# X loads as single SyncE transfers, four issued at the start, and the gate matrix loaded into its blocks

## The chip, the core and the metric

The kernel runs on one core of a Trainium2 chip. The core has five engines that run their own instruction streams and wait for each other by semaphores: TensorE (PE) for matmuls, VectorE (DVE), ScalarE (ACT), GpSimd (POOL) and SyncE (SP). SP, ACT and POOL can issue DMA transfers; 16 DMA engines of the core carry them out. PE, DVE and the other engines take their instructions in program order, so an instruction that waits holds back all that stand behind it on its engine.

The metric is the device time of one execution in microseconds (us), as a median of several runs. "Granted clock" is the share of full TensorE clock that the chip gave.

## The reference

The input x has 8 sequences of 3584 positions with 192 channels (28672 tokens). A causal convolution with seven taps per head comes first, its taps a softmax of a small weight; then a routed feed-forward network with 8 experts, in which tokens go to experts greedily by their logits, each expert taking exactly 3584:

```python
w = softmax(weight, axis=-1)                       # 8 heads x 7 taps
out = np.einsum('hk,bskhg->bshg', w, x_unf)        # causal: six zeros ahead of each sequence
x = out.reshape(B * S, D)
logits = x @ w_gate                                # 28672 x 8
order = np.argsort(-logits.flatten())
# walk the order: a token takes expert e if it has none yet and e has room
for e in range(E):
    h = np.maximum(x[assigned == e] @ w1[e], 0.0)
    out[assigned == e] = h @ w2[e]
```

## The kernel before

The convolution is done in 16 half batches (`NHB`) of 1792 positions. A half batch's input is the tile X: 118 partitions by 16 windows by 192 channels in float32. Partitions 6 to 117 hold the 112 positions of each window, partitions 0 to 5 the six positions ahead of it (the halo). For each of 8 heads `conv` multiplies X by a banded 118 x 128 matrix `TH`, which `toeplitz` builds from the softmaxed taps on DVE, ACT and POOL at the start; PE writes the product into one of four PSUM banks (`cv`), ACT copies it into the tile `a` (three buffers), and ACT then issues the store of `a` to `attn` in DRAM (L205).

X has four buffers. `load(i)` (L183) fetches half batch i: on POOL a memset of the first window's halo where a sequence begins, on SP the halo (L189 or L192), and then the 112 positions in two halves of eight windows each (L194). Windows 0 to 7 are issued by SP, windows 8 to 15 by ACT (by SP for half batch 0). A load waits until the convolution that read its buffer is done. In the main loop `load(i + 3)` stands ahead of `conv(i)`, so ACT meets the issue of its half ahead of the evictions of half batch i.

The gate: DVE transposes `a` into `aT` (`transp`), PE multiplies it by the gate matrix (`logits`, six steps of four matmuls, two steps at a time under the name `gate`), and ACT copies the result, after a transpose on PE, into `LT` (`logits_t`). The gate matrix lies in GF (shown as c_mu in the profile): 128 partitions by 6 blocks of 32 columns, in which the 32 partitions of quarter pb use columns 8 pb to 8 pb + 7 and the rest is zero. `gate_ops` (L167) loads the matrix four times into `wgr` with one transfer for each quarter, sets GF to zero on POOL, and copies the quarters in with four POOL copies (L173).

The order of work is written out by hand. Inside `conv(i)`, after each head's matmul, `mid(h)` takes one piece from a list: in half batch 2 and later these are, in turn, a quarter of the transposes of half batch i - 1 and two logits steps of half batch i - 2. So the first gate matmuls stand on PE after the second head of half batch 2. On SP the order at the start is: taps, load 0, load 1 (the call inside `toeplitz`, after the exponential, so that ACT's half comes behind it), the four gate transfers, load 2, and from the main loop load 3, load 4 and so on. On POOL the constants of `r.consts()` stand behind the four copies into GF.

From the fourth half batch on, the threshold search and the routing of tokens run on DVE and PE between the convolutions; when lists of tokens exist, POOL gathers rows of `attn` and the feed-forward network begins. It fills the rest of the time, with PE as its main engine.

Of the kernel before, what the change touches and what calls it, by code (L numbers as in the profile page):

```python
# [6 lines left out]
F32 = mybir.dt.float32  # L7
# [8 lines left out]
NE, D, NTOK, F, CAP = 8, 192, 28672, 1024, 3584  # L16
W, HW_, NHB = 112, 16, 16
# [97 lines left out]
def build(ctx, tc, nc, x, weight, wg, attn, LT, wk):  # L115

    k = K()
    k.nc = nc
    k.tc = tc
    V, A, PE, P = nc.vector, nc.scalar, nc.tensor, nc.gpsimd  # L120
    cst = ctx.enter_context(tc.tile_pool(name="cst", bufs=1, side="right"))


    wb = cst.tile([128, 8, 7], F32, name="wb")
    nc.sync.dma_start(wb, bass.AP(tensor=weight.tensor, offset=weight.offset, ap=[[0, 128], [7, 8], [1, 7]]))
    pmi = cst.tile([128, 128], I32, name="pmi")
    P.iota(pmi, pattern=[[-1, 128]], base=0, channel_multiplier=1)
    D0 = cst.tile([128, 128], BF, name="D0")
    V.tensor_copy(D0, pmi)
    TH = cst.tile([128, 8, 128], F32, name="TH")  # L130
    P.memset(TH[:, :, W:128], 0.0)
    MK = cst.tile([128, 7, W], BF, name="MK")
    for j in range(7):
        V.tensor_scalar(MK[:, j], D0[:, 0:W], float(j), None, op0=OP.is_equal)
    wm = cst.tile([128, 8], F32, name="wm")

    def toeplitz():
        V.tensor_reduce(wm, wb, axis=AX.X, op=OP.max)
        V.tensor_tensor(wb, wb, wm[:, :, None].to_broadcast([128, 8, 7]), op=OP.subtract)
        A.activation(wb, wb, AF.Exp)  # L140
        load(1)
        V.tensor_reduce(wm, wb, axis=AX.X, op=OP.add)
        V.tensor_scalar(wm, wm, 1e-9, None, op0=OP.add)
        V.reciprocal(wm, wm)
        V.tensor_tensor(wb, wb, wm[:, :, None].to_broadcast([128, 8, 7]), op=OP.mult)

        tk = cst.tile([128, 2, W], F32, name="tk")
        for h in (1, 5):
            A.activation(TH[:, h, 0:W], MK[:, 0], AF.Copy, scale=wb[:, h, 0:1])
            for j in range(1, 7):  # L150
                A.activation(tk[:, j % 2], MK[:, j], AF.Copy, scale=wb[:, h, j:j + 1])
                P.tensor_tensor(TH[:, h, 0:W], TH[:, h, 0:W], tk[:, j % 2], op=OP.add)
        for hs in ((0, 2), (3, 4), (6, 7)):
            for j in range(7):
                for h in hs:
                    t = TH[:, h, 0:W]
                    if j == 0:
                        V.tensor_scalar(t, MK[:, 0], wb[:, h, 0:1], None, op0=OP.mult)
                    else:
                        V.scalar_tensor_tensor(t, MK[:, j], wb[:, h, j:j + 1], t, op0=OP.mult, op1=OP.add)  # L160


    wgr = cst.tile([128, 6, 8], F32, name="wgr")
    GF = wk.tile([128, 6, 32], F32, name="c_mu")
    pm = wk.tile([128, 1], F32, name="pm")

    def gate_ops():  # L167
        for pb in range(4):
            nc.sync.dma_start(wgr[32 * pb:32 * pb + 32], wg.rearrange("(c f) e -> f c e", f=32))
        P.memset(GF, 0.0)  # L170
        for pb in range(4):
            q = slice(32 * pb, 32 * pb + 32)
            P.tensor_copy(GF[q, :, 8 * pb:8 * pb + 8], wgr[q])  # L173

        pi = cst.tile([128, 1], I32, name="pi")
        P.iota(pi, pattern=[[0, 1]], base=0, channel_multiplier=1)
        V.tensor_scalar(pi, pi, 24, None, op0=OP.bitwise_and)
        V.tensor_scalar(pm, pi, 24.0, -1.0, op0=OP.is_equal, op1=OP.mult)


    X, AT, AA = {}, {}, {}

    def load(i):  # L183
        t = X[i] = k.xp[i % 4].tile([118, 16, D], F32, name="X")
        b, hf = divmod(i, 2)
        o = x.offset + (b * 3584 + hf * 1792) * D
        if hf == 0:
            P.memset(t[0:6, 0], 0.0)
            nc.sync.dma_start(t[0:6, 1:16], bass.AP(tensor=x.tensor, offset=o + (W - 6) * D,  # L189
                                                    ap=[[D, 6], [W * D, 15], [1, D]]))  # L190
        else:
            nc.sync.dma_start(t[0:6], bass.AP(tensor=x.tensor, offset=o - 6 * D, ap=[[D, 6], [W * D, 16], [1, D]]))  # L192
        for eng, w in ((nc.sync, 0), (A if i else nc.sync, 8)):
            eng.dma_start(t[6:118, w:w + 8], bass.AP(tensor=x.tensor, offset=o + w * W * D, ap=[[D, W], [W * D, 8], [1, D]]))  # L194

    def conv(i, mid):
        t = X.pop(i)
        a = AA[i] = k.ap[i % 3].tile([128, 16, D], F32, name="a")
        o = a.rearrange("p w (h c) -> p h w c", c=24)
        for h in range(8):  # L200
            ps = k.cps.tile([128, 512], F32, name="cv")
            PE.matmul(ps[:, 0:384], TH[0:118, h], t[:, :, h * 24:(h + 1) * 24], start=True, stop=True)
            mid(h)
            A.activation(o[:, h], ps[:, 0:384].rearrange("p (w c) -> p w c", c=24), AF.Copy)
        A.dma_start(attn[i * 1792:(i + 1) * 1792].rearrange("(g p b) d -> p g (b d)", g=4, b=4),  # L205
                    a[0:W].rearrange("p (g b) d -> p g (b d)", b=4))

    def transp(i, u):

        if u == 0:  # L210
            AT[i] = [k.hp[i % 2].tile([128, 16, 6, 32], F32, name="aT")]
        V.transpose(AT[i][0][:, 4 * u:4 * u + 4].rearrange("p w c t -> p (w c t)"),
                    AA[i][:, 4 * u:4 * u + 4].rearrange("p w d -> p (w d)"))
        if u == 3:
            AA.pop(i)

    def logits(i, u):

        if u == 0:
            AT[i].append(k.bank("pl"))  # L220
        pl = AT[i][-1]
        for c in range(4):
            w = slice(4 * c, 4 * c + 4)
            PE.matmul(pl[32 * c:32 * c + 32, 0:128], GF[:, u], AT[i][0][:, w, u], start=(u == 0), stop=(u == 5))
        if u == 5:
            L = AT[i] = k.lrow()
            l, m = (t.rearrange("p (w t) -> p w t", t=32) for t in (L, pl[:, 0:128]))
            A.activation(l[:, :, 0:16], m[:, :, 0:16], AF.Copy)
            A.activation(l[:, :, 16:32], m[:, :, 16:32], AF.Identity, bias=pm)

    def logits_t(i):
        L = AT.pop(i)
        pt = k.bank("pt")
        PE.transpose(pt[:, 0:128], L, k.ident)
        v = pt[:, 0:128].rearrange("p (b q e) -> p e b q", q=4, e=8)
        o = LT[:, :, 16 * i:16 * i + 16].rearrange("p e (b q) -> p e b q", q=4)
        A.activation(o, v, AF.Copy)

    k.load, k.conv, k.transp, k.logits, k.logits_t = load, conv, transp, logits, logits_t
    k.toeplitz, k.gate_ops = toeplitz, gate_ops  # L240
    return k

# [1241 lines left out]
def moe_kernel(ctx, tc, x, weight, wg, w1, w2, out):  # L1484
    nc = Pace(tc.nc)
    V, P = nc.vector, nc.gpsimd
# [4 lines left out]
    with ExitStack() as cw:  # L1491
# [71 lines left out]
        ff.xg = pool(cw, "fg", 2)  # L1563
        ff.xs = pool(cw, "fx", 2)
        k = build(cs, tc, nc, x, weight, wg, attn, LT, wk)
        k.ident = r.ident
        lp = pool(cs, "lp", 2, **right)
# [41 lines left out]
                for _ in range(2):  # L1609
                    todo.pop(0)()  # L1610

        k.load(0)
        k.toeplitz()
        k.gate_ops()
        k.load(2)
        r.consts()
        for i in range(NHB):
            if i + 3 < NHB:
                k.load(i + 3)
            if i == 4:  # L1620
                r.consts_late()
            if i == 13:
                cx[0].close()
                for _ in range(4):
                    ff.wload()
                ff.wpool(cw, 0, **late)

            def mid(h):

                if i and h == 0:  # L1630
                    if i >= LAG:
                        left.append(partial(gates, i - 2))
                    for u in range(4):
                        left.append(partial(k.transp, i - 1, u))
                        if 1 < i and (u == 3 or i < LAG):
                            left.append(partial(gate, i - 2, u) if u < 3 else partial(end, i - 2))
                for _ in range(2 if got else 1):
                    if left and (i < LAG or got):
                        left.pop(0)()
                if i >= 14 and h % 2:  # L1640
                    ff.wsplit(-1, P)
                hook(8 * i + h)

            k.conv(i, mid)
# [88 lines left out]
```

## Time and profile before

| What | Value |
|---|---|
| Time, median of 3 runs | 1236.66 us (1236.03 to 1237.11) |
| Profiled execution | 1234.62 us |
| Its span, first to last instruction | 1232.9 us |
| Mean granted clock | 0.998 |
| DMA traffic | 182.03 MB, mean 148 GB/s |

The profile is of one execution. Its page gives each engine's busy time and share of the span; "PEld" is PE's weight load, which overlaps PE. The strip of 40 slices gives busy shares in tenths. A row of the timeline reads: start, duration, engine, line, operation, out <- in, shape, how many were merged into the row, and in brackets how long the engine sat idle before it and what ended that wait. SPq and ACTq are the queues from which SP and ACT issue transfers; the duration of such a row is that of the issue, not of the transfer. Many lines are recorded as L56, a helper through which DVE, ACT and PE are called, so instructions are told apart by their tiles.

### The profile page before, as it was taken

How to read it: one execution, taken by the hardware profiler on the slowest of the kernel's cores; microseconds unless marked ns; L12 is line 12 of the kernel's file. 1: busy time of each engine (PE TensorE's matmuls, PEld its weight loads, DVE VectorE, ACT ScalarE, POOL GpSimd, SP SyncE). 2: the span in 40 equal slices, each digit the busy share in tenths (PEclk: the TensorE clock that was granted, in tenths of full speed). 3: DMA queues.
4: the chain of work that ended last, by engine and by line, in shares of the span. 5: the costliest groups of instructions: out<-in, count | busy, mean ns of one | idle time of the engine just before them, and what ended most of it. 6: DMA issues, size and time to landing. Idle time of an engine off the chain costs nothing.

```text
span 1232.9 us, 21779 instructions
## 1 busy us (share of the span) xinstructions
PE 1201.0 (97%) x7694; PEld 1034.1 (84%) x7694; DVE 983.1 (80%) x2117; ACT 565.6 (46%) x1252; POOL 540.3 (44%) x528
## 2 busy tenths in 40 slices
PE   4999999999999999999999999999999999999997
PEld 2445678899989988889888889999999999999997
DVE  7398789898998988899979866777777777777762
ACT  4454565556445455454554443333433343334332
POOL 3000344444546555545455435444444544543422
PEclk9999999999999999999999999999999999999999
DMA  9999674659427474655343432114323232423100
GB/s 239 347 344 326 230 223 123 176 158 312 153 59 220 133 246 129 219 159 190 88 132 114 116 106 74 49 40 152 108 91 105 97 107 89 159 72 120 49 24 28
DMA packets 129221, 182.03 MB, mean 148 GB/s; under 512 B 21632, under 2 KB 91728, under 8 KB 127440
## 3 DMA queue, kind: packets, MB, share of 16 engines
q1 hardware_dynamic: 86496, 104.15, 27.3%
q0 software_dynamic: 21504, 44.07, 12.0%
q10 hardware_dynamic: 21104, 32.34, 7.8%
q8 instruction: 62, 1.02, 0.4%
q14 instruction: 55, 0.45, 0.1%
HBM read 102.38 MB, written 78.12 MB: 146 GB/s over the span
## 4 chain that ended last, share of the span: by engine, by line
PE 91%; DVE 4%; DMA 2%; ACT 1%; issue 1%; POOL 0%; SPq 0%; ACTq 0%; POOLq 0%; DVEq 0%
PE ph L56 42%; PE y L56 41%; PE cv L56 3%; PE bg L56 3%; DMA X<-in_x_dram 1%; DVE aT L56 1%; PE pl L56 1%; DMA wgr<-in_moe_w_gate_dram 1%; DVE X L56 1%; PE px L56 0%; ACT a L56 0%; ACT X L56 0%; POOL c_mu L173 0%; SPq L194 0%; DVE hl L56 0%
## 5 line engine op out<-in xcount | busy, mean ns | idle before, releaser
L56 PE MATMUL y<-w,hh 128*128 128x384 f32 x1792 | 535.8, 355 | 0.0
L56 ACT ACTIVATE hh<-ph 128x512 fp32r<-128x512 f32 x448 | 268.0, 598 | 470.8 <-PE ph L56 467.9
L56 PE MATMUL y<-w,hl 128*128 128x192 f32 x1792 | 449.0, 251 | 0.0
L56 DVE SCALAR_TENSOR_TENSOR hl<-ph,hh 128x512 fp32r<-128x512 f32 x448 | 307.9, 687 | 133.3 <-ACT hh L56 127.4
L56 PE MATMUL ph<-xa,w 128*128 128x512 f32 x1344 | 395.0, 402 | 0.0
L56 PEld LDWEIGHTS y<-w,hl 128*128 128x128 f32 x1792 | 340.9, 190 | 16.3
L56 PEld LDWEIGHTS y<-w,hh 128*128 128x128 f32 x1792 | 336.3, 188 | 19.8 <-issue 1.7
L1367 POOL DMA_INDIRECT out_dram<-yo,ia x128 | 145.4, 1136 | 211.5 <-DVE yo L56 180.6
L56 PEld LDWEIGHTS ph<-xa,w 128*128 128x128 f32 x1344 | 218.4, 189 | 20.3 <-issue 1.2
L1367 POOL DMA_INDIRECT out_dram<-yo,ib x96 | 96.0, 1000 | 220.0 <-DVE yo L56 212.6
L56 PE MATMUL ph<-xd,w 128*128 128x512 f32 x448 | 177.7, 397 | 1.2 <-DVE xd L56 1.2
L56 PE MATMUL ph<-xd,dl 128*128 128x512 f32 x448 | 174.2, 389 | 0.3 <-DVE dl L56 0.3
L56 DVE STREAM_TRANSPOSE xs<-xg 32x128 f32<-32x128 f32 (+2 forms) x408 | 164.8, 404 | 6.6
L1292 POOL DMA_INDIRECT xg<-attn,ja x128 | 140.6, 1098 | 46.2 <-issue 40.7
L56 ACT ACTIVATE yt<-y 128x192 f32<-128x192 f32 x224 | 73.2, 327 | 94.3 <-PE y L56 91.7
L56 PE MATMUL cv<-X,TH 118*128 118x384 f32 x256 | 99.5, 517 | 17.3 <-DVE TH L56 12.7
L1292 POOL DMA_INDIRECT xg<-attn,jb x96 | 103.5, 1078 | 29.3 <-issue 29.0
L56 DVE TENSOR_TENSOR yo<-y,yt 128x192 f32<-128x192 f32 x224 | 79.3, 354 | 42.8 <-ACT yt L56 40.2
L56 PEld LDWEIGHTS ph<-xd,w 128*128 128x128 f32 x448 | 84.0, 188 | 21.5 <-DVE xd L56 1.7
L56 PEld LDWEIGHTS ph<-xd,dl 128*128 128x128 f32 x448 | 84.2, 188 | 19.9 <-issue 0.5
L56 PEld LDWEIGHTS cv<-X,TH 118*128 118x128 f32 x256 | 45.1, 195 | 47.7 <-issue 12.5
L56 ACT ACTIVATE a<-cv 128x384 f32<-128x384 f32 x128 | 59.2, 493 | 47.4 <-PE cv L56 23.0
(238 smaller groups left out, 918.0 us busy)
## 6 DMA issues: line engine op xcount, KB each, us to landing
attn<-a ACTq DMA_DIRECT2D x16, 1344.0 KB, 10.2
X<-in_x_dram SPq DMA_DIRECT2D x17, 672.0 KB, 14.3
raw<-in_moe_w_dram SPq DMA_DIRECT2D x56, 192.0 KB, 4.0
X<-in_x_dram ACTq DMA_DIRECT2D x15, 672.0 KB, 10.5
kw<-w SPq DMA_DIRECT2D x36, 256.0 KB, 4.3
kv<-w SPq DMA_DIRECT2D x24, 384.0 KB, 5.7
scr<-xs SPq DMA_DIRECT2D x96, 96.0 KB, 2.6
w<-kw SPq DMA_DIRECT2D x6, 1536.0 KB, 7.2
```

The lines of the kernel that those rows point to most:

```text
L56: return f(*a, **k)
L1292: self.nc.gpsimd.indirect_dma_start(out=t[:, b], out_offset=None, in_=self.attn[0:rows], in_offset=bass.IndirectOffsetOnAxis(ap=idx[b], ax ...
L1367: st = self.nc.gpsimd.indirect_dma_start(out=self.out, out_offset=bass.IndirectOffsetOnAxis(ap=idx, axis=0), in_=o, in_offset=None, bounds ...
```

## The change

Three things change. A half batch's 112 positions are one transfer of 16 windows, issued by SP, in place of two of eight; ACT issues no load of X any more. Loads 0 to 3 are issued one behind the other before `toeplitz`; in the loop, load 4 comes first, at i = 1. The gate matrix is transferred straight into GF's four blocks, behind the memset of GF; the tile `wgr` and the POOL copies are gone. The four transfers have the same sizes as before and stand on SP behind the four loads.

```diff
@@ toeplitz
         A.activation(wb, wb, AF.Exp)
-        load(1)
         V.tensor_reduce(wm, wb, axis=AX.X, op=OP.add)
@@ gate_ops
-    wgr = cst.tile([128, 6, 8], F32, name="wgr")
     GF = wk.tile([128, 6, 32], F32, name="c_mu")
     pm = wk.tile([128, 1], F32, name="pm")
 
     def gate_ops():
-        for pb in range(4):
-            nc.sync.dma_start(wgr[32 * pb:32 * pb + 32], wg.rearrange("(c f) e -> f c e", f=32))
         P.memset(GF, 0.0)
         for pb in range(4):
-            q = slice(32 * pb, 32 * pb + 32)
-            P.tensor_copy(GF[q, :, 8 * pb:8 * pb + 8], wgr[q])
+            nc.sync.dma_start(GF[32 * pb:32 * pb + 32, :, 8 * pb:8 * pb + 8],
+                              wg.rearrange("(c f) e -> f c e", f=32))
@@ load
-        for eng, w in ((nc.sync, 0), (A if i else nc.sync, 8)):
-            eng.dma_start(t[6:118, w:w + 8], bass.AP(tensor=x.tensor, offset=o + w * W * D, ap=[[D, W], [W * D, 8], [1, D]]))
+        nc.sync.dma_start(t[6:118], bass.AP(tensor=x.tensor, offset=o, ap=[[D, W], [W * D, 16], [1, D]]))
@@ moe_kernel
-        k.load(0)
+        for i in range(4):
+            k.load(i)
         k.toeplitz()
         k.gate_ops()
-        k.load(2)
         r.consts()
         for i in range(NHB):
-            if i + 3 < NHB:
+            if 0 < i and i + 3 < NHB:
                 k.load(i + 3)
```

## The prediction

> **What bounds the kernel now.** I read the page first, then busy time by stage, then the first 60 us row by row.
>
> ```profile
> span 1232.9 us, 21779 instructions
> PE 1201.0 (97%) x7694; PEld 1034.1 (84%) x7694; DVE 983.1 (80%) x2117; ACT 565.6 (46%) x1252; POOL 540.3 (44%) x528
> DMA  9999674659427474655343432114323232423100
> ```
>
> PE works 97% of the span, in program order. A shift of its early work that is not swallowed by a later wait therefore reaches the end at its full size. The change touches the loads of X and the gate matrix only, and these belong to the first stage, where the DMA engines are busy in nine tenths and more. The table by stage says where PE has time to lose there:
>
> ```profile
> 10.00:20.00 10.00, 7.28 (x16) 3.67 (x17) 8.97 (x32) 4.92 (x12) 4.79 (x12) 1.00 1.13 238
> 20.00:30.00 10.00, 7.30 (x22) 3.78 (x20) 7.77 (x15) 4.38 (x10) 2.78 (x17) 0.95 1.09 290
> 30.00:40.00 10.00, 10.00 (x84) 5.28 (x84) 1.98 (x3) 4.00 (x11) 1.78 (x3) 0.88 1.07 359
> 40.00:50.00 10.00, 8.12 (x68) 4.25 (x67) 4.40 (x7) 3.98 (x11) 0.00 (x0) 1.00 1.06 339
> 50.00:60.00 10.00, 10.00 (x87) 5.03 (x85) 5.41 (x7) 6.24 (x16) 0.25 (x1) 1.00 1.05 344
> ```
>
> The columns are the stretch, its length, busy us of PE, PEld, DVE, ACT and POOL, the granted clock, the DMA share and GB/s. PE is short in 10 to 30 and in 40 to 50; in 20 to 40 the clock is granted at 0.95 and 0.88, which is 0.5 + 1.2 = 1.7 us of full clock missing. The PE timeline, then the merged one, name the waits:
>
> ```profile
> 11.51 6.15 PE L56 MATMUL cv<-X,TH 118*128 118x384 f32 x12 [11.51 <-DVE TH L56]
> 18.87 6.69 PE L56 MATMUL cv<-X,TH 118*128 118x384 f32 x20 [1.21 <-DVE TH L56]
> 28.26 2.21 PE L56 MATMUL cv<-X,TH 118*128 118x384 f32 x4 [2.70 <-DMA X<-in_x_dram]
> ```
>
> ```profile
> 30.40 1.08 PE L56 MATMUL pl<-aT,c_mu 128*32 128x128 f32 x16
> ...
> 33.33 2.04 ACT L56 ACTIVATE a<-cv 128x384 f32<-128x384 f32 x5 [7.24 <-DMA attn<-a]
> ...
> 42.93 2.02 ACT L56 ACTIVATE a<-cv 128x384 f32<-128x384 f32 x5 [4.57 <-DMA X<-in_x_dram]
> ...
> 43.47 1.56 PE L56 MATMUL cv<-X,TH 118*128 118x384 f32 x4 [1.88 <-ACT a L56]
> ...
> 48.42 0.65 PE L56 MATMUL pl<-aT,c_mu 128*32 128x128 f32 x16
> ```
>
> Half batches 0 and 1 wait for TH alone and end at 18.87 + 6.69 = 25.56. Half batch 2 then waits 2.70 us for X. At 28.4 ACT stands still until 33.33, and again before 42.93: the next thing in its order is the issue of the other half of an X load, and that waits for an earlier transfer. The second of these stops PE by 1.88 us. One ACT copy into LT closes each half batch of logits, so these rows are the milestones:
>
> ```profile
> 37.70 0.28 ACT L56 ACTIVATE LT<-pt 128x128 f32<-128x128 f32 x1 [0.27 <-PE pt L56]
> 47.24 0.28 ACT L56 ACTIVATE LT<-pt 128x128 f32<-128x128 f32 x1 [0.26 <-PE pt L56]
> 54.83 0.28 ACT L56 ACTIVATE LT<-pt 128x128 f32<-128x128 f32 x1 [0.27 <-PE pt L56]
> 62.41 0.28 ACT L56 ACTIVATE LT<-pt 128x128 f32<-128x128 f32 x1 [0.27 <-PE pt L56]
> ```
>
> An undisturbed half batch takes 54.83 - 47.24 = 7.59 us, and 7.58 again; the one that ends at 47.24 took 9.54. In an undisturbed one it is 54.83 - 48.42 = 6.41 us from the first gate matmul (pl) to the copy. From 47.24 on I take the rest of the kernel as a fixed train.
>
> **Removed and moved, part by part.**
>
> ```profile
> 5.14 6.02 SPq L169 DMA_DIRECT2D wgr<-in_moe_w_gate_dram  x4
> ...
> 12.76 0.26 POOL L170 MEMSET c_mu<- 128x192 f32 x1
> ...
> 16.60 0.27 SPq L189 DMA_DIRECT2D X<-in_x_dram  x1
> ...
> 17.18 0.31 SPq L194 DMA_DIRECT2D X<-in_x_dram  x1
> 17.54 0.46 SPq L192 DMA_DIRECT2D X<-in_x_dram  x1
> 17.57 2.30 POOL L173 COPY c_mu<-wgr 32x48 f32<-32x48 f32 x4 [4.56 <-DMA wgr<-in_moe_w_gate_dram]
> ...
> 18.04 0.57 SPq L194 DMA_DIRECT2D X<-in_x_dram  x1
> ...
> 20.48 3.87 SPq L189 DMA_DIRECT2D X<-in_x_dram  x1
> ...
> 20.96 0.32 ACTq L205 DMA_DIRECT2D attn<-a  x1
> ```
>
> Loads 2 and 3 on SP now stand behind four gate transfers and a wait until 16.60; with the change all four loads are issued first. Load 2 then moves ahead of load 3 and of the gate matrix. Its SP half lands at 28.26 today, when PE takes it. How early can it be?
>
> ```profile
> DMA packets 8198, 5.51 MB, mean 213 GB/s; under 512 B 1105, under 2 KB 8197, under 8 KB 8197
> ...
> X<-in_x_dram SPq DMA_DIRECT2D x3, 67.5 KB
> ```
>
> ```profile
> DMA packets 728, 0.55 MB, mean 238 GB/s; under 512 B 15, under 2 KB 728, under 8 KB 728
> ```
>
> ```profile
> DMA packets 1211, 1.91 MB, mean 375 GB/s; under 512 B 28, under 2 KB 775, under 8 KB 1211
> ...
> q1 hardware_dynamic: 571, 0.43, 29.4%
> ```
>
> These are answers on the DMA queues for 0 to 25.9 us, for 16.5 to 18.8 and for 25.9 to 31 (q1 is SP's). A load is two halves of 672 KB and a halo of 67.5 or 72 KB, 1.45 MB; four are 5.79 MB. At 238 GB/s and a start near 2.6 us, three loads (4.34 MB) need 18.2 us: load 2 is there by 21 to 24 us, before PE ends half batch 1 at 25.56. **The wait of 2.70 us goes.** The two stops of ACT go as well, since no X transfer is left in its order. Alone, this would put the two half batches up to the second LT copy at 25.56 + 1.5 (two heads) + 6.41 + 7.59 = 41.1 instead of 47.24, **6.2 us earlier**.
>
> **What is late next: the gate matrix.** Its four transfers stood ahead of loads 2 and 3 and landed at 17.5, 13 us before their first use at 30.40. Now they stand behind all four loads on SP's queue. The first logits come after two heads of half batch 2, at 25.56 + 1.5 = 27.05, and PE takes everything in order: until GF is there it stands. So the time t at which GF lands decides. From below: in 0 to 25.9 us the kernel moved 5.51 of the 5.79 MB, and the store of half batch 0 (1344 KB, issued 20.96) not yet. The remaining 0.28 MB then ran beside that store at 0.43 MB in 5.1 us, 84 GB/s, so some 3 us more: 29, and with the landing 30. Without any store in front it would be 28. From the landings:
>
> ```profile
> DMA to landing us min/median/max: 11.9/11.9/11.9
> ```
>
> ```profile
> 24.40 18.04 DMA X<-in_x_dram
> ```
>
> The first row is that store alone: 20.96 + 11.9 = 32.9. The second, of the chain of waits, is the next SP load behind load 3, which lands at 42.4. Load 2's half landed at 28.2, so load 3's lies between 28 and 42; the middle is 35. I take **t = 33.5**, next to the store's 32.9, and keep 28 and 37 as ends.
>
> The Trainium skill, "DMA: Bandwidth & Descriptors", section "Why a DMA increments its semaphore by 16 and not by 1", speaks against the change here. By it a transfer from SP runs on as many engines, up to 16, as divide its slowest dimension: 16 for 112 or 32 partitions, 6 for a halo's 6 rows. Six engines would then hold the halo packets of four loads in addition, and a piece of GF behind them. Its estimate here, with rows of 768 bytes and 52 ns each (16 engines at 238 GB/s): 62 rows or 3 us later on those six; by it t is 31 without a store in front and 34 with one. No view here shows single engines, so t stays as chosen.
>
> With a PE wait from 27.05 to 33.5 the clock falls too. Nearest row: after the idle 2.70 us 1.7 us of full clock were missing. I take 1.7; it may be 0 if GF comes early. The same skill, "TensorE: Matmul & The Clock Gate", section "Part 1: The HAM clock gate (the "warmup" mystery)", has half rate after an idle window of about 3.4 us, and 3.4 us of half rate are those 1.7; the trace agrees.
>
> **The sum.** Second LT copy: 33.5 + 6.41 + 7.59 + 1.7 = 49.2 against 47.24, **+2.0 us**.
>
> ```profile
> 96.84 1.89 ACTq L194 DMA_DIRECT2D X<-in_x_dram  x1
> ```
>
> ```profile
> 6.45 5.46 DVE L56 SCALAR_TENSOR_TENSOR TH<-MK,wb,TH 128x112 f32<-128x112 bf16 x12
> ...
> 15.95 3.03 DVE L56 SCALAR_TENSOR_TENSOR TH<-MK,wb,TH 128x112 f32<-128x112 bf16 x12
> ```
>
> Later ACT loses such issues too (1.89 us at 96.84, ahead of an eviction). PE has four banks in hand, so most is hidden; I count -0.5, between 0 and -1.9. The four POOL copies (2.30 us and a wait of 4.56) go, and POOL's constants move from 20 us to 13. There they run beside TH: DVE's TH step took 455 ns (5.46 / 12) beside POOL's additions and 253 without. One to two us of POOL work can cost TH 0 to 1 us, hidden while PE waits for GF; if GF is early it counts. ACT's store of half batch 1 may have to wait for an earlier transfer until about t; its evictions then start near t, when PE has used two of four banks, so nothing is added. Loads 4 on, issued as buffers come free, have about 9 us in hand (load 4's half lands at 42.4 and half batch 4 starts at 47).
>
> In total +1.5 us: 1234.6 becomes 1236.1 for the profiled execution, which lies 2.0 below the median of 1236.66; on the median **1238.2**. In short the change is t - 32.0 us.
>
> **Rivals.**
> 1. *GF lands early* (t below 29.5): the loads run without the store in front, as 5.51 MB by 25.9 us would let them. Against: the store is issued at 20.96, before load 3 ends. At t = 28.5 the clock loss is about 0 and the result is 28.5 + 14.0 - 47.24 - 0.5 = -5.2, 1231.5; at 29.5 it is -2.5, 1234.2. Chance 0.19.
> 2. *GF lands later than the store* (t above 34.5): load 3's tail and GF get turns only beside stores, at 84 GB/s; for it speaks the load that took 18.04 us. At t = 36.5 it is +4.5, 1241.2; it decides from 34.5 on. Slower. Chance 0.26.
> 3. *The change doesn't reorder*: SP is held by earlier transfers (5.14 + 6.02, then until 16.60), so loads 2 and 3 start no earlier and GF lands last all the same; it ends like 2, near 1241, and is in its chance.
>
> My forecast (t 29.5 to 34.5, 1234.2 to 1239.1) has 0.55. A measurement of this kernel can tell about 0.2%, 2.5 us, from no change. The range 1232.3 to 1241.0 leaves out 0.1 on either side, by t from 28.7 to 36.3. Faster 0.19, same 0.55, slower 0.26.
>
> **What would show it.** Half batch 2's first matmuls near 25.6 without a wait for X; a PE wait ended by GF's transfer at the first pl near 33.5, with half clock after it; no ACT wait behind an X issue; the second LT copy near 49.2. Wrong if pl follows at 27 (then the copy is near 41 to 43), if X is still waited for at 28, or if a later stage takes back what the LT copies show.

## The result: 0.96% slower, and the profile after

The changed kernel takes **1248.85 us** (median of 5 runs, 1246.97 to 1249.32) beside 1236.39 us for the kernel before on the same chip (5 runs, 1235.63 to 1237.11). The ratio on record is 1.0096, with a 95% interval of 1.0084 to 1.0107 (dividing the two medians gives 1.0101, inside it). I had forecast 1238.2 us with a range to 1241.0, so the change is slower by more than the whole range allowed. "Before" and "after" are the two kernels below; GF is the gate matrix in its blocks, shown as c_mu.

The page of after says where the traffic went. Its rows: the span, and the DMA queues with packets (rows of a transfer), MB and share of 16 engines' time:

```profile
span 1245.2 us, 21734 instructions
...
q1 hardware_dynamic: 99920, 114.47, 31.4%
...
q10 hardware_dynamic: 7424, 22.02, 4.6%
```

The span is 12.3 us longer than before's 1232.9. SP's queue (q1) carries 114.47 MB; the 22.02 MB on ACT's queue (q10) are the 16 stores of `attn` alone (16 times 1344 KB). Next the timeline of PE in the first 45 us, then that of SP and ACT:

```profile
19.12 8.27 PE L56 MATMUL cv<-X,TH 118*128 118x384 f32 x24 [0.42 <-DVE TH L56]
39.88 1.08 PE L56 MATMUL pl<-aT,c_mu 128*32 128x128 f32 x16 [12.49 <-DMA c_mu<-in_moe_w_gate_dram]
```

```profile
19.14 13.96 SPq L168 DMA_DIRECT2D c_mu<-in_moe_w_gate_dram  x4
...
21.20 0.35 ACTq L200 DMA_DIRECT2D attn<-a  x1
...
26.36 0.31 ACTq L200 DMA_DIRECT2D attn<-a  x1
```

The first row runs through half batch 1 into the first two heads of half batch 2 without a stop: the wait of 2.70 us for X is gone. Then PE stands 12.49 us, until GF lands at 39.88. Both stores (at 21.20 and 26.36) were issued without a stop, 0.35 and 0.31 us each, in front of the last gate pieces, and the issue of the four gate transfers itself took 13.96 us. The table by stage shows the price of the idle time in the clock (columns as above):

```profile
30.00:40.00 10.00, 0.12 (x4) 0.15 (x8) 0.00 (x0) 0.00 (x0) 0.00 (x0) 0.55 1.02 314
40.00:50.00 10.00, 10.00 (x77) 5.15 (x80) 1.19 (x2) 3.80 (x10) 1.59 (x3) 0.77 1.02 193
```

From 40 to 50 the clock is 0.77, so 2.3 us of full clock are missing there. The milestones are the second and the eleventh LT copy and the first matmul of the experts (ph), from the timelines of ACT and PE. First after:

```profile
56.09 0.28 ACT L56 ACTIVATE LT<-pt 128x128 f32<-128x128 f32 x1 [0.27 <-PE pt L56]
...
134.63 0.28 ACT L56 ACTIVATE LT<-pt 128x128 f32<-128x128 f32 x1 [0.27 <-PE pt L56]
...
167.78 0.94 PE L56 MATMUL ph<-xa,w 128*128 128x512 f32 x3
```

and before, whose second copy is at 47.24:

```profile
126.12 0.28 ACT L56 ACTIVATE LT<-pt 128x128 f32<-128x128 f32 x1 [0.26 <-PE pt L56]
...
155.62 0.94 PE L56 MATMUL ph<-xa,w 128*128 128x512 f32 x3
```

The second copy is 56.09 - 47.24 = **8.85 us** later, the eleventh 8.51, ph 12.16, the span 12.3. So two losses make the result: 8.85 us at GF, and 12.16 - 8.51 = **3.65 us** between the eleventh copy and the experts. The chain of work that ended last names the second (first two rows, after), and the timeline of PE shows it as a wait (third row):

```profile
133.29 14.98 DMA raw<-in_moe_w_dram
...
157.41 8.32 DMA xg<-attn,ja
```

```profile
165.78 0.51 PE L56 MATMUL bg<-ident,xg 128*128 128x128 f32 x2 [3.50 <-DMA xg<-attn,ja]
```

These are the experts' weights (raw) and the first gather of tokens (xg), behind the weights' preparation on POOL. SP issues the first raw transfer at 133.29; before it did at 116.00:

```profile
116.00 1.10 SPq L1219 DMA_DIRECT2D raw<-in_moe_w_dram  x1
```

### The profile page after: what moved, and what is told of

Same layout as the page of the kernel before. It is cut to its first block, busy times and chain, and to the rows that moved or that the text cites. A ratio compares the mean times of both kernels' runs of the same rounds, so it can differ in the third digit from the quotient of the medians.

```text
span 1245.2 us, 21734 instructions
## 1 busy us (share of the span) xinstructions
PE 1202.3 (97%) x7694; PEld 1034.5 (83%) x7694; DVE 981.3 (79%) x2117; ACT 566.5 (45%) x1252; POOL 537.8 (43%) x524
## 3 DMA queue, kind: packets, MB, share of 16 engines
q1 hardware_dynamic: 99920, 114.47, 31.4%
q10 hardware_dynamic: 7424, 22.02, 4.6%
## 4 chain that ended last, share of the span: by engine, by line
PE 89%; DVE 5%; DMA 4%; issue 1%; ACT 1%; POOL 0%; SPq 0%; POOLq 0%; ACTq 0%; DVEq 0%
PE ph L56 42%; PE y L56 40%; PE cv L56 3%; PE bg L56 3%; DMA raw<-in_moe_w_dram 1%; DVE aT L56 1%; DVE X L56 1%; DVE TH L56 1%; PE pl L56 1%; DMA attn<-a 1%; DMA xg<-attn,ja 1%; DMA c_mu<-in_moe_w_gate_dram 1%; PE px L56 0%; DMA wb<-in_weight_dram 0%; SPq L189 0%
```

## The experiments

The edits are against the kernel named in each. All ratios are to before, run in the same group on the same chip; in the groups of e5 to e8 and of e17, e18 before itself took 1245 to 1247 us, so times aren't compared between groups, ratios are.

### GF early: e1, e2, e3

e1 takes GF's lateness away: the memset of GF and the four transfers stand behind load 0.

```diff
         for i in range(4):
             k.load(i)
+            if i == 0:
+                k.gate_load()      # memset of GF, four gate transfers
         k.toeplitz()
-        k.gate_ops()               # with the gate transfers
+        k.gate_ops()               # without them
```

> The changed kernel with the four gate transfers (and the memset of GF) moved from behind load 3 to behind load 0. Theory: the late gate matrix cost 8.8 us (second LT copy at 56.09 in place of 47.24), and a second loss of about 3.6 us comes later, where the expert weights arrive late behind SP's loads. Then the first gate matmul follows at about 27.4 with no wait, the second LT copy stands near 41.5, and the time is 1236.4 - 5.7 + 3.6 = about 1234. Rival: the loads themselves are too slow on one queue, PE then waits for load 3 or 4 where it waited for GF, the second LT copy stays above 50 and the time above 1243.

Measured: 1245.05 us, ratio 1.0073 (1.0055 to 1.0091). GF was no longer waited for, yet the second LT copy came at 49.90. In place of GF it is load 3, for half batch 3, that PE waits for (timeline of PE, e1):

```profile
39.28 2.90 PE L56 MATMUL cv<-X,TH 118*128 118x384 f32 x4 [4.93 <-DMA X<-in_x_dram]
```

GF's place in the queue therefore explains only a part. Whatever holds back GF holds back the loads as well.

e2 keeps the change, but loads 4 on go back to two halves, on SP and ACT:

```diff
+        if i < 4:
             nc.sync.dma_start(t[6:118], ...)          # 16 windows
+            return
+        for eng, w in ((nc.sync, 0), (A, 8)):
+            eng.dma_start(t[6:118, w:w + 8], ...)     # 8 windows
```

> The changed kernel, but from load 4 on a half batch comes again as two halves, the second issued by ACT; loads 0 to 3 stay single transfers on SP. Theory: the later loss of 3.6 us comes from SP's queue, which carries all loads and holds the expert weights back (their first issue at 133.3 in place of 116.0); with half the load on ACT the first weight issue is within 10 us behind that of before, the wait of 3.5 us for xg goes, and the time is 1248.9 - 3.6 = about 1245; the wait of 12.5 us for GF stays. Rival: the weights are late only because the whole first stage is late; then the time stays at 1249.

1247.5 us, 1.0099 (1.0081 to 1.0117). The first raw issue moves from 133.29 to 126.54 (timeline of SP, e2):

```profile
126.54 1.33 SPq L1218 DMA_DIRECT2D raw<-in_moe_w_dram  x1
```

The wait for xg is gone, and from the eleventh copy to ph it is 166.16 - 136.66 = 29.50 us, exactly before's 155.62 - 126.12. So the later 3.65 us come from loading X over the one queue. The ratio gains nothing: in the profiles ph is 1.62 us earlier than after's (166.16 against 167.78), as GF came even later (first pl at 41.36 instead of 39.88), and that much the ratios don't tell apart.

e3 has both edits.

> Both edits at once: gate transfers behind load 0, and halves on SP and ACT from load 4 on. Theory: both losses go and the start is 5.7 us earlier than before: 1236.4 - 5.7 = about 1231, below both kernels; ACT's waits ahead of its half loads may return and cost up to 2 us. Rival, one of the losses has another cause: 1234 or more.

1241.69 us, 1.0048 (1.0031 to 1.0064): the wait for GF and the later loss are gone (29.47 us from the eleventh copy to ph), but X of half batch 3 is still 3.61 us late at 38.34, and ACT's stops are back.

### One part at a time: e4 to e8

e4 is before with the single transfer alone, on SP.

```diff
-        for eng, w in ((nc.sync, 0), (A if i else nc.sync, 8)):
-            eng.dma_start(t[6:118, w:w + 8], ...)
+        nc.sync.dma_start(t[6:118], ...)
```

> The kernel before, with one part of the change alone: a half batch's 112 positions are one transfer on SP, in the order of before, gate copies as before. Theory: the queue on SP makes the expert weights late by several us (+3.6) and ACT's two stops go (-1.9): about 1238. Also load 2 stands behind the gate transfers on SP, so half batch 2 waits for X until 28 or later. Rival: which queue carries the second half makes no difference to the weights; then about 1235.

1243.15 us, 1.0056 (1.0039 to 1.0073). More than half of the loss is in this part alone. Timeline of PE, then the answers on the DMA queues for 30 to 34 us and for 44 to 49 us:

```profile
38.17 2.90 PE L56 MATMUL cv<-X,TH 118*128 118x384 f32 x4 [4.61 <-DMA X<-in_x_dram]
```

```profile
q10 hardware_dynamic: 483, 1.43, 88.8%
q1 hardware_dynamic: 250, 0.19, 14.0%
```

```profile
DMA packets 1360, 1.03 MB, mean 206 GB/s; under 512 B 19, under 2 KB 1360, under 8 KB 1360
```

While a store is under way, the loads get 0.19 MB in 4 us, 47 GB/s. When it has passed, the loads run alone, at 206 GB/s. The total swings between some 400 and 206.

e5 is the change with halves everywhere; e6 is before with the gate straight into GF; e7 is e4 with the transfer split in two again, both on SP; e8 has whole transfers, even half batches on SP, odd ones on ACT.

```diff
# e6, in before's place
+        P.memset(GF, 0.0)
         for pb in range(4):
-            nc.sync.dma_start(wgr[32 * pb:32 * pb + 32], ...)
+            nc.sync.dma_start(GF[32 * pb:32 * pb + 32, :, 8 * pb:8 * pb + 8], ...)
-        P.memset(GF, 0.0)          # and the four POOL copies
# e7
+        for w in (0, 8):
+            nc.sync.dma_start(t[6:118, w:w + 8], ...)
# e8
+        (A if i % 2 else nc.sync).dma_start(t[6:118], ...)
```

> The changed kernel with every half batch as two halves again, the second on ACT (on SP for half batch 0): the four early loads and the direct gate transfer stay. Theory of the order: the gate transfers stand last behind four loads and a store, whatever the size of the loads; then the first gate matmul stays near 36 to 39, the second LT copy near 53 to 56, and the time at 1243 to 1246. Rival, the single transfers make the loads slow: the gate matrix lands by 33, the second LT copy near 48, about 1237.

> The kernel before with the direct gate transfer alone: the four transfers go into GF's blocks in the place of the old ones, behind the memset of GF at 13. Theory: the matrix is in place by about 20, its first use is at 30.4, and SP waits until 16.6 anyway: 1236.5, within 1 us. Rival: the later issue on SP pushes loads 2 and 3 back by 3 us or more, half batch 2 starts at 30 or later, 1238 to 1240.

> The kernel before, with both halves of eight windows issued by SP, one behind the other. It tells apart why the single transfer alone came to 1243.2. Theory of the queue: one queue carries all loads, its issues are held until earlier loads are in, and less is in flight: the time is again about 1243, with waits for X at half batch 3 and later. Rival, the size: a transfer of 16 windows is slow in itself; then halves on SP give about 1236.

> The kernel before, with one transfer of 16 windows for a half batch, issued by SP for even and by ACT for odd half batches. Theory of the queue: two queues share the load again, so the waits for X go and the time is 1235 to 1238. Rival, the size: about 1243 again.

| Kernel | Time, us | Ratio | 95% interval |
|---|---|---|---|
| e5 | 1254.98 | 1.0076 | 1.0056 to 1.0096 |
| e6 | 1247.95 | 1.0019 | 1.0008 to 1.0030 |
| e7 | 1253.11 | 1.0057 | 1.0040 to 1.0074 |
| e8 | 1247.58 | 1.0019 | 1.0007 to 1.0031 |

e7 equals e4: two small transfers on SP cost what one large one does. e8 has the large transfers and gives two thirds of the loss back. So it isn't the size of the transfer but **which queue** the loads stand in. e5 never waits for GF, but PE begins only at 21.78 instead of 11.51. ACT's halves of three more loads stand beside load 0: from 2 to 10 us SP's queue, with load 0 in it, moved 417 rows and ACT's 1514. That PE waits for load 0 is argued from this, as the trace names DVE; so e5 doesn't separate the theories. In e6 SP can issue the gate only after POOL's memset (at 12.72 instead of 5.14), and load 2 behind it comes late (SP's half is issued at 18.19 instead of 17.18):

```profile
30.16 2.90 PE L56 MATMUL cv<-X,TH 118*128 118x384 f32 x4 [4.11 <-DMA X<-in_x_dram]
```

### What stands in front of GF: e9, e10, e12

e9 is the change with the stores of half batches 0 and 1 issued behind half batch 2; e10 is the change without the halo transfers of loads 1 to 3, so that part of the convolution at the borders of windows is left out; e12 is before with the gate straight into GF, the memset early and load 2 ahead of the gate.

```diff
# e9: conv
-        A.dma_start(attn[i * 1792:(i + 1) * 1792]..., a[0:W]...)
+        ST.append((i, a))
+        while ST and i > 1:
+            j, s = ST.pop(0)
+            A.dma_start(attn[j * 1792:(j + 1) * 1792]..., s[0:W]...)
# e10: load, and P.memset(X[i][0:6], 0.0) for i in 1 to 3 behind gate_ops
+        if 0 < i < 4:
+            pass
-        if hf == 0:
+        elif hf == 0:
# e12
         load(1)
+        load(2)
...
         k.gate_ops()
-        k.load(2)
```

> The changed kernel with the stores of half batches 0 and 1 issued only behind half batch 2, so that no store is in front of the gate transfers. Looked at: the start of the first gate matmul, 39.9 in the changed kernel. Theory: two stores of 1344 KB, each some 3.5 us of all DMA engines, were served ahead of load 3's tail and of the gate matrix, where I had counted one; without them it starts at 32 to 34. Rival: four loads on one queue take that long by themselves; then 37 or later. The total is no aim here, since half batch 3 then waits for the late stores.

> The changed kernel without the halo transfers of loads 1 to 3, whose six partitions are set to zero on POOL instead; this leaves out part of the computation at the borders of windows of those half batches. Looked at: the first gate matmul. If the halos' rows lie on a few of the 16 DMA engines, and these finish last, 47 rows of about 52 ns go from the slowest ones and it starts 2.5 us or more earlier, at 37 or below. If the halos are spread evenly (216 of 5655 KB), it moves by less than 1 us.

> A version that is meant to beat both: the kernel before with halves on both queues, the gate matrix straight into GF (memset of GF first of all), and only load 2 moved ahead of the gate transfers, its second half issued by ACT behind that of load 1. Theory: half batch 2 starts at 25.6 without a wait for X, the gate matrix is there by 25, ACT's stops remain, the second LT copy is 2 to 4 us earlier than before: ratio 0.997 to 0.9985. Rival: load 3 is later for it, half batch 3 waits, and the ratio is 1.000 or more.

In e9 the gate comes 39.88 - 34.22 = 5.7 us earlier (timeline of PE). The second row is e9's strip of busy DMA engines in tenths, 40 slices of 20 to 30 us:

```profile
34.22 1.08 PE L56 MATMUL pl<-aT,c_mu 128*32 128x128 f32 x16 [6.50 <-DMA c_mu<-in_moe_w_gate_dram]
```

```profile
DMA  9999999999999999999999999999999999864543
```

The two stores thus cost GF 5.7 us. And even with no store at all in flight, the engines are busy for only three to five tenths from 29 to 30 us. That the end of the loads and the gate hang on a few engines would fit this; no view shows single engines. In total e9 gains nothing (1248.92 us, a single run), as the held stores come all at once and ACT waits for them later.

e10 has no wait for GF at all. Answers on the DMA queues for 2 to 20 us, of after and of e10:

```profile
DMA packets 5166, 3.86 MB, mean 214 GB/s; under 512 B 172, under 2 KB 5166, under 8 KB 5166
```

```profile
DMA packets 5794, 4.34 MB, mean 241 GB/s; under 512 B 176, under 2 KB 5794, under 8 KB 5794
```

and for 30 to 40 us of after, 20 to 30 us of e10:

```profile
DMA packets 3005, 3.14 MB, mean 314 GB/s; under 512 B 850, under 2 KB 2370, under 8 KB 3005
...
q10 hardware_dynamic: 667, 1.95, 48.2%
```

```profile
DMA packets 3397, 2.99 MB, mean 299 GB/s; under 512 B 869, under 2 KB 2953, under 8 KB 3396
```

The gate matrix is the only large group of pieces below 512 bytes in these stretches (4 times 32 x 6 pieces of 32 bytes, 768 in all; a few others are always there), so the count of those packets shows when it moved: in e10 before 30 us, in after nearly all behind 30, together with 1.95 MB of stores. Without the halos the loads ran at 241 GB/s instead of 214 and at 20 us only some 1.2 of their 5.6 MB were left, against 1.9 of 5.8 in after; these and the gate were through before 30 us, ahead of the second store. With the halos the loads were not through when the two stores came, and the gate's pieces moved beside and behind the stores. The gain is far more than the expected 2.5 us. But e10 is no clean test of the halos: its memsets hold POOL for 8.12 us, PE waits 3.44 us for TH, and the stores are issued at 23.05 and 29.90 instead of 21.20 and 26.36. How much of it is due to the halos, and how much to the later stores, is open. e10's time is 1241.29 us (a single run); from the eleventh copy to ph it is 161.93 - 129.34 = 32.6 us, so the later loss remains.

e12 takes 1242.66 us, 1.0046 (1.0031 to 1.0060): with load 2 ahead of the gate PE waits for ACT's evictions instead, 4.92 us at 27.86. ACT stands 6.42 us until 27.32: ahead of those evictions it has the store of half batch 0 to issue, at 23.56, and its half of load 4, at 26.95, which by the chain of waits was held by its half of load 3 (issued at 11.58).

### Rows of the stores: e11, e13 to e16

A store row has 3072 bytes (four windows of a position), a load row 768 bytes. e11 is e4 with stores in rows of 768 bytes. It leaves the index of the gather as it was, so that the experts get other tokens' rows.

```diff
-        A.dma_start(attn[i * 1792:(i + 1) * 1792].rearrange("(g p b) d -> p g (b d)", g=4, b=4),
-                    a[0:W].rearrange("p (g b) d -> p g (b d)", b=4))
+        A.dma_start(attn[i * 1792:(i + 1) * 1792].rearrange("(w p) d -> p w d", w=16), a[0:W])
```

> The kernel with single transfers on SP alone (1.0056 of the time before), with stores whose rows in DRAM are 768 bytes in place of 3072; the rows of attn then stand in another order, so that the gathers fetch other positions. Theory: stores take turns with loads row by row, a store row is four load rows, so a store passes quickly and the loads then run alone, at 215 to 250 GB/s, where mixed with stores the total is 340 to 375; with equal rows they mix longer and the waits for X shrink: ratio 1.000 to 1.003. Rival: one queue of loads is slow whatever stands beside it: 1.005 or more.

1232.33 us, 0.9955 (0.9939 to 0.9972): faster than before, where e4 was 0.56% slower. From e13 on the index for the gather goes with the order (the token's own number, which takes two short DVE instructions fewer a list, not three as the expectation says):

```diff
-        V.scalar_tensor_tensor(y, i, -127.0 / 4, x, op0=OP.mult, op1=OP.add)
...
-        V.scalar_tensor_tensor(y, gi, 28.0, y, op0=OP.mult, op1=OP.add)
...
-        V.scalar_tensor_tensor(y, i, 4.0, y, op0=OP.mult, op1=OP.add)
+        V.scalar_tensor_tensor(y, i, -80.0, x, op0=OP.mult, op1=OP.add)
...
-            V.tensor_scalar(row, y, 4.0, None, op0=OP.mult)
+            V.tensor_scalar(row, y, 0.0, None, op0=OP.max)
```

e13 is before, e14 after, e15 e4 and e16 e3, each with these small rows.

> Before, with attn kept in the order of the tokens: a half batch's store has 1792 rows of 768 bytes in place of 448 of 3072, and the index for the gather is the token's own (three short DVE instructions fewer in each list). Theory R (row by row turns): before's loads ride half on SP's and half on ACT's queue, where the stores stand in order with them, and its traffic from 30 to 120 us already ran at 340 GB/s; so little is to be had: ratio 0.996 to 1.000, 30 to 120 us at 335 to 350 GB/s, the wait of 2.70 us for X at half batch 2 gone or changed by up to 2 us. Theory Q (the one queue): before has no such queue and the rows do nothing: 0.999 to 1.001. A price of small rows (1792 descriptors of 768 bytes for a store): slower, 1.001 to 1.006, and the store's landing some us later.

> The whole change with the same small store rows and matching indices. Theory R: the two stores no longer go ahead of the four loads and the gate transfers whole, so GF lands a few us earlier (first pl without a wait or with under 8 us, where it was 13.40 to 14.66), traffic from 30 to 120 us back from 303 to 330 GB/s or more, LT copy 10 to first ph back from 35.3 to 31.7 us; ratio 0.996 to 1.003. Theory Q: first pl at 39 to 40 and the later 3.65 us stay: 1.008 to 1.010.

> e11 again (before with the single transfer on SP, small store rows), now with indices to match, so that the expert stage gathers the rows that the reference asks for. Theory R: as e11, ratio 0.994 to 0.998, 30 to 120 us at about 341 GB/s, second LT copy at about 45. If e11's gain came from its other gathers in the expert stage: 1.002 to 1.006, as e4, with the stage before 140 us as in e11.

> The change with the gate transfers behind load 0, loads 4 on as halves on SP and ACT (as e3, 1.0048) and the small store rows with matching indices. Theory R: its X wait at half batch 3 (3.61 us) and ACT's stops shrink, ratio 0.994 to 1.000. Theory Q: as e3, 1.003 to 1.006.

| Kernel | Loads | Large rows | Small rows, ratio (interval) |
|---|---|---|---|
| before, e13 | halves on SP and ACT | 1 | 1.0144 (1.0126 to 1.0162) |
| after, e14 | whole on SP, four first | 1.0096 | 1.0037 (1.0023 to 1.0051) |
| e4, e15 | whole on SP | 1.0056 | **0.9938** (0.9925 to 0.9952) |
| e3, e16 | halves from load 4 on | 1.0048 | 1.0176 (1.0154 to 1.0198) |

Where the loads stand on SP alone, small rows win 0.6 to 1.2%. Where half of them stand on ACT's queue with the stores, small rows lose 1.3 to 1.4%. Answers on the DMA queues of e15 for 30 to 34 us, the stretch shown for e4 above:

```profile
DMA packets 1923, 1.48 MB, mean 369 GB/s; under 512 B 20, under 2 KB 1922, under 8 KB 1922
...
q1 hardware_dynamic: 961, 0.73, 53.9%
q10 hardware_dynamic: 961, 0.73, 53.8%
```

961 rows of loads and 961 rows of the store in the same 4 us: here the queues take turns **row for row**. Not in every stretch: from 28 to 30 us it was 275 rows of loads to 700 of the store, and in e4's stretch above 250 to 483. What sets the turns there is open; from 30 to 120 us e15 has 20974 rows of loads to 19880. With equal rows the loads get half here, 0.73 MB in 4 us or 183 GB/s, and the engines are hardly ever left with loads alone: the two queues together still move 347 GB/s over 30 to 120 us. A load row takes an engine 0.539 * 16 * 4 us / 961 = 36 ns here; in e4's stretch of loads alone it was 62 ns (1.054 * 16 * 5 us / 1360, its q1 had 105.4%). A half batch's load and store (2.75 MB without the halo) thus need 7.5 us at 369 GB/s, just the 7.59 us that PE takes for one. In e4 they need 1.38 MB at 358 GB/s for the store (1.43 MB in 4 us) and, after the 0.18 MB that pass beside it, 1.2 MB at 206: by this estimate 9.7 us. That is more than PE's pace, and the loads fall behind until PE's own half batches grow to some 10 us.

e14 shows which loss goes: GF is still waited for, 12.16 us until 39.81, but from the eleventh copy to ph it is 163.00 - 133.89 = 29.11 us again. In e15 it is 28.89 us, so the other index is worth at most 0.6 us there; its second copy is at 40.79, 6.45 us ahead of before's (timeline of ACT, e15):

```profile
40.79 0.28 ACT L56 ACTIVATE LT<-pt 128x128 f32<-128x128 f32 x1 [0.27 <-PE pt L56]
```

The Trainium skill, "DMA: Bandwidth & Descriptors", section "Queues, rings and completion order", says that each engine goes round the queues for which it has work, a packet of several descriptors at a time; the equal counts of 30 to 34 us agree, the 275 to 700 of 28 to 30 us don't show it. The same page of the Trainium skill, "Issuing engines are not separate DMA queues", says that issuing from several engines saves only issue time; here e7 and e8, with 1.0057 and 1.0019, differ by more than that, and the measurement decides.

e13 answers the other half. Timeline of ACT, and the list of PE's waits in the first 180 us:

```profile
21.29 5.82 ACTq L194 DMA_DIRECT2D X<-in_x_dram  x1
27.16 1.64 ACT L56 ACTIVATE a<-cv 128x384 f32<-128x384 f32 x4 [6.58 <-DMA X<-in_x_dram]
```

```profile
PE cv L56 <- ACT a L56: 18.9, 8, 5.1
```

ACT's issue of its half of a load takes 5.82 us right behind the store of half batch 0. The same row of before:

```profile
21.40 0.43 ACTq L194 DMA_DIRECT2D X<-in_x_dram  x1
```

That is 0.43 us. The store's 1792 rows in place of 448 stand ahead of it in ACT's own queue. ACT's evictions wait meanwhile, and PE for them, 18.9 us in eight waits. That the queue has no room left for so many rows is argued from this, not shown.

### What is left of the change: e17, e18

e17 is e1 with small rows; e18 is e15 with e6's gate.

> The change with the gate transfers behind load 0 (as e1) and the small store rows with matching indices (as e14). If GF's place and the rows of the stores are the whole loss: no wait for GF, LT copy 10 to first ph 29 us, ratio 0.992 to 0.998, as e15. If the order of the four loads, begun ahead of all, costs something of its own (load 3 lands late, X waits as the 4.93 us in e1): second LT copy at 47 or later, ratio 0.999 to 1.004.

> e15 (single transfers on SP, small store rows, before's order) with the gate transfers straight into GF behind its memset, in before's place. If the direct transfers do harm by themselves (e6: +0.19%, half batch 2 waits 4.11 us for X as the memset holds SP back): 0.995 to 0.998. If small store rows cover it: 0.993 to 0.995.

e17: 1240.28 us beside 1246.64, 0.9953 (0.9938 to 0.9967). e18: 1239.38 us, 0.9947 (0.9934 to 0.9960). In e17 half batch 2 waits 3.27 us for X, and the second copy is at 45.56. Timeline of PE and of ACT, e17:

```profile
28.51 1.53 PE L56 MATMUL cv<-X,TH 118*128 118x384 f32 x4 [3.27 <-DMA X<-in_x_dram]
```

```profile
45.56 0.28 ACT L56 ACTIVATE LT<-pt 128x128 f32<-128x128 f32 x1 [0.27 <-PE pt L56]
```

All of the change's edits are in e17, with the gate's transfers moved and the stores in other rows, and it is 0.47% faster than before. So with GF's place and the rows of the stores altered, nothing of the loss is left. (From the eleventh copy to ph e17 and e18 have 32.4 us instead of 29.5, but so do e6 and e8, with 33.0, on runs where before was slower too; there is no profile of before from those, so the reason is open.) The order of the four loads, and the gate without its POOL copies, show no gain of their own: e15, which has neither, has the lowest ratio, though the three intervals overlap.

## Why the prediction was wrong, point by point

**"The wait of 2.70 us goes", and the two stops of ACT.** Right as rows: half batch 2 begins without a wait, and no eviction waits behind an issue of X. But that this alone would bring the second copy forward by 6.2 us, to 41.1, failed. e1 and e4 have these waits gone (but for 0.92 us in e1) and still reach the second copy at 49.90 and 48.98: half batch 3's X is then 4.93 and 4.61 us late, and the matmuls behind that wait are slow (2.90 us for the first two heads, where 1.5 is usual). What I took for a mere loss of ACT was also what let the loads keep up, by my reading of e4, e7 and e8: ACT's half of each load stood in the queue of the stores, in order with them.

**"I take t = 33.5", the term that was mis-sized first.** GF landed at 39.88, 6.4 us later. Three things were off in it. I took 238 GB/s for the loads, from 2.3 us of before in which ACT's queue alone ran, with halves and no halo; SP's queue with the halos in it moved 214, and so the loads were not through when the stores came. I counted one store in front, "next to the store's 32.9", and held that the second "may have to wait for an earlier transfer until about t"; both were issued without a stop, and e9 gives them 5.7 us together. And I left the halos out of t for lack of a row; without them, though with later stores too, e10 has GF there before 30. Rival 2 had this mechanism ("load 3's tail and GF get turns only beside stores"), but I worked it at 36.5, ended the bounds at 37, and gave it 0.26.

The Trainium skill's estimate that I quoted, 3 us for the halos on six engines ("DMA: Bandwidth & Descriptors", "Why a DMA increments its semaphore by 16 and not by 1"), was the right direction: e9's strip falls to three to five tenths from 29 to 30 us, as busy as about 6 engines of 16 would be. I wrote that it gave 34 with one store in front; my own 30 and 3 make 33, and the run had two stores. e9 with none had 34.22 where it gave 31.

**The half clock, 1.7 us.** 39.88 + 6.41 + 7.59 would be 53.88; the copy was at 56.09, so 2.2 us: right in kind, 0.5 short.

**"From 47.24 on I take the rest of the kernel as a fixed train."** This is the step that failed outright. With -0.5 us counted for ACT's later issues, 8.85 became 8.51 at the eleventh copy, as said. But after it 3.65 us more were lost, because the weights of the experts stand on SP's queue behind the loads of X, and with one queue these were late: first raw at 133.29. e2, with halves in the loop, takes exactly this part away. That loads 4 on "have about 9 us in hand" didn't follow from the numbers beside it, either: from 42.4 to 47 it is 4.6 us, and that with before's two queues.

The sum, from the forecast of +1.5 us: 6.4 for GF, 0.5 for the clock, 0.2 for the later issues, 3.65 for the weights make 12.2 us, and the span grew by 12.3.

**POOL's constants beside TH, 0 to 1 us.** PE's stretch of the later heads began at 19.12 instead of 18.87: 0.25 us, within the bounds, and hidden by the wait for GF.

## What to carry to other kernels

When transfers move from two queues to one, don't carry over a rate from a quiet stretch: ask beside which rows each queue's rows will run. Where the loads have a queue to themselves, try store rows as short as theirs; here that won 0.6 to 1.2%. A step that is moved behind large transfers on a queue is late by everything that other queues put in front of those, so count every store that can be issued by then, not only the next. And before calling the rest of a kernel a fixed train, follow the same queue to its next user, here the weights 90 us later.

## What the runs showed of the hardware

How two queues share the DMA engines goes by the length of their rows: with equal rows 961 to 961 in 4 us, 0.73 MB each (e15, though not in every stretch), with store rows four times as long 250 to 483, 0.19 MB to 1.43 (e4). Loads of 768-byte rows alone run at 206 to 214 GB/s with their halos (62 ns a row in e4), beside equally long store rows at 36 ns a row and 369 GB/s together, so that a stretch with loads alone is the slow one. Small store rows help or harm by the queue they stand in: 0.9938 with the loads elsewhere (e15), 1.0144 with half of the loads behind them on ACT's queue (e13), where an issue then lasts up to 5.84 us. And the halos, 5% of a load's bytes (67.5 or 72 of some 1416 KB), took the loads from 241 (e10) to 214 GB/s (after), both from 2 to 20 us.
